# Block 0's queries in slots of the weight ring, and new durations in the planner of a fused attention and two-MLP kernel

## The chip, the cores and the metric

The kernel runs on one core of one Trainium2 chip. The time of a kernel is its device time in microseconds (us). Engines are named as in the profile: PE is TensorE (matmuls), DVE is VectorE, ACT is ScalarE, POOL is GpSimd, and SP is the queue that issues most DMAs.

## What is computed

Eight batches of eight heads attend to keys and values that are pooled eight to one; the result, 4608 tokens of 512 columns, goes through two MLPs.

```python
# q, k, v: (8, 8, 576, 64)
k_p = k.reshape(B, H, Sp, pool, D).mean(axis=3)          # Sp = 72, pool = 8
v_p = v.reshape(B, H, Sp, pool, D).mean(axis=3)
attn = softmax(scale * q @ k_p^T)                        # sum + 1e-9
x = (attn @ v_p), heads side by side                     # (4608, 512)
h = x @ w_in                                             # 512 -> 2048
g = where(h >= 1, h, where(h <= -1, 0, (h + 1)**2 / 4))
x = g @ w_out                                            # 2048 -> 512
out = (sigmoid(x @ w_gate) * (x @ w_val)) @ w_out2       # 512 -> 1536 -> 512
```

## The kernel before

The weights of the MLPs come as 64-bit floating-point numbers. The kernel reads them as pairs of 32-bit words, makes float32 of them on ACT and DVE (`weight`), and splits every operand of a main matmul into a high and a low float32r part. `three` multiplies high by high, high by low and low by high, so one product of a 128 x 128 tile with 512 columns is three matmuls.

The tokens are nine blocks of 512 (`j`). Attention is done per block and pair of heads (`unit(j, p)`, four pairs); `pooled(b, p)` makes the pooled keys and values of batch b. For block 0 the keys and values are summed on PE and the queries are transposed on PE (lines 384 to 389); for the later blocks queries come in 32 x 32 pieces by many small DMAs and are transposed on DVE (lines 395 and 401).

The first MLP runs as 144 steps, nine blocks of 16 column tiles of w_in (`M1`). A step makes h (12 matmuls), then g on ACT and DVE (lines 645 to 649, then `high_part` and `low_part`, lines 505 and 514), then adds to four accumulators (12 matmuls). During block 0 the weights arrive and are converted: a tile of w_in is loaded into a slot of the ring "win" (16 slots), converted through f, and its two float32r parts take another slot of "win"; a tile of w_out is loaded into the ring "raw" (two slots) and kept as float32, and split again in each step (`wj`). The attention of block j + 1 is done during block j. The second MLP follows: block 0 in a plain way, with the weights combined into seven sums and differences on the side, and the other eight blocks in four pairs with seven products for eight. Their due times go by `S2` and `PSTEP`.

Nothing is issued in the order of the code. Every instruction, or small group, is recorded with `op(engine, cost, key, function, r=, w=)`: the engine or the engines that could do it, its duration in us, a due time (the key), and the buffers that it reads and writes. `Plan.issue` then runs a list scheduler over them while the program is built: it follows its own clock, lets an engine start what is ready, of several that are ready within 0.05 us the one with the lowest key, gives an operation that two engines could do to the one that would end it first, and takes a slot of a ring for a buffer when one is free by that clock. A DMA lasts, in the plan, by its `nbytes` at 360 GB/s behind the ones before it, with at most eight under way. What comes out is the fixed order of each engine's queue; on the chip every queue works in that order and waits for semaphores.

So the costs decide the order of the queues and which of ACT and DVE does a copy; they do not decide what is computed. Keys for the steps are `due1(s) = 30 + 6.35 s`. The load of w_in's tile m has the key due1(m) - 0.1 - 23.19, that of w_out's tile m due1(m + 1) - 2.73 - 23.19. In block 0, pair p of the attention has T = 2.02 p; its k and q loads have the key T - 20, its v load T + 10.09. The pairs of block 1 have T = due1(2), due1(4), due1(7), due1(10), each less 6.12, and their k and q loads the key T - 20.

Buffers of a ring are recorded by `Buf`; one with `fifo=False` need not take its slot in the recorded order. In the kernel before the four q tiles of block 0 and those of all later blocks share the ring "q", which has two slots:

```python
qs = buf_a("q", 2, [P, NT4, 2, D])        # block 0, line 376
qs = buf_a("q", 2, [P, TB // 32, 32])     # later blocks, line 391
```

Of the kernel before, what the change touches and what calls it, by code (L numbers as in the profile page):

```python
# [18 lines left out]
P = 128  # L19
# [177 lines left out]
def pooled_attention_two_mlps(  # L197
# [92 lines left out]
    T0, S1, S2 = START, STEP1, 7.8  # L290

    def due1(s):
        return T0 + S1 * s
# [69 lines left out]
    def unit(j, p, T):  # L363
# [53 lines left out]
        for h in range(2):  # L417
# [4 lines left out]
            op(DVE, 0.37, T + 4, lambda view=view, mx=mx: nc.vector.tensor_reduce(  # L422
# [16 lines left out]
        if first:  # L439

            flat = Src(aT, lambda t: t.rearrange("c a h t j -> c (a h t j)"))
            for h in range(2):
# [9 lines left out]
                op((ACT, DVE), (0.48, 0.6), T + 10, (  # L452
                    lambda copy=copy: copy(nc.scalar.copy),
                    lambda copy=copy: copy(nc.vector.tensor_copy)), r=[pt], w=[aT])
        else:
            aq = buf_a("aq", 1, [P, 3, 2, NT4 * 32])
            for h in range(2):
                op(DVE, 0.47, T + 9, lambda h=h: nc.vector.transpose(
                    out=aq.t[:, :, h].rearrange("p b (t j) -> p t b j", t=NT4),
                    in_=e.t[:, :, h].rearrange("p t (b i) -> p t b i", i=32)), r=[e], w=[aq])  # L460
# [28 lines left out]
        op((ACT, DVE), (0.48, 0.6), T + 19 - AHEAD_PX * first, (  # L489
# [3 lines left out]
        op(DVE, 0.6, T + 19 - AHEAD_PX * first, lambda: nc.vector.scalar_tensor_tensor(  # L493
# [8 lines left out]
    def high_part(key, dst, src, eng=None):  # L502

        ways = {
            ACT: (0.52, lambda: nc.scalar.copy(out=dst.t[:, 0], in_=src())),  # L505
            DVE: (0.34, lambda: nc.vector.tensor_copy(out=dst.t[:, 0], in_=src())),
            PL: (0.59, lambda: nc.gpsimd.tensor_scalar(
                out=dst.t[:, 0], in0=src(), scalar1=1.0, scalar2=1.0, op0=ALU.mult, op1=ALU.mult))}
        engs = eng or HI
        op(engs, [ways[e][0] for e in engs], key, [ways[e][1] for e in engs], r=[src.b], w=[dst])  # L510

    def low_part(key, dst, src, eng=None):
        engs = eng or LO
        op(engs, [0.6 if e == DVE else 1.23 for e in engs], key, [lambda e=e: by[e].tensor_tensor(  # L514
# [12 lines left out]
    def weight(w, m, cols, r, key, t=None, keep=None, spill=None):  # L527
# [23 lines left out]
        op(ACT, 0.52, key - 7, lambda: nc.scalar.activation(out=f.t, in_=high().bitcast(F32), func=AF.Abs),  # L551
           r=[r], w=[f])
        a = op(ACT, 0.52, key - 6, lambda: nc.scalar.activation(
            out=low().bitcast(I32), in_=low(), func=AF.Copy, scale=2.0 ** -29), r=[r])
# [3 lines left out]
        op(DVE, 0.34, key - 5, lambda: nc.vector.tensor_scalar(  # L558
            out=f.t.bitcast(U32), in0=f.t.bitcast(U32), scalar1=3, scalar2=0x3FFFFFF8,
            op0=ALU.logical_shift_left, op1=ALU.bitwise_and), r=[f], w=[f])  # L560
        op(DVE, 0.6, key - 5, lambda: nc.vector.scalar_tensor_tensor(
# [22 lines left out]
    def columns(key, o, w, xs):  # L584
        last = []
        for c in range(KD):
# [30 lines left out]
    for j in range(NB):  # L617
        xs = xs_of.pop(j)
        for m in range(M1):
# [39 lines left out]
            for c in range(KD):  # L659
# [3 lines left out]
                last_y[c] = [op(PE, 0.65, due1(s + 2) + 2.6 + 0.1 * c, mm, r=[wj, g], w=[accs[c]], behind=last_y[c])]  # L663
# [45 lines left out]
    PSTEP = 11 * 2.6  # L709
# [20 lines left out]
    def prepare(n, i, key):  # L730
# [19 lines left out]
        def comb(o, x, y, alu):  # L750
            op2(DVE, 0.38, key - 4, lambda: nc.vector.tensor_tensor(out=sm.t[:, o], in0=x(), in1=y(), op=alu),
# [27 lines left out]
    def out_part(gs, m, key, accs, last, ahead=5):  # L779
# [5 lines left out]
        for c in range(4):  # L785
# [3 lines left out]
            last[c] = [op(PE, 0.65, key + 0.1 * c, mm, r=[w, g], w=[accs[c]], behind=last[c])]  # L789
# [13 lines left out]
    for i in range(MP):  # L803
# [3 lines left out]
        for n in range(2):  # L807
            sl, a21 = slots[n]
            for f in range(2):
                last = []  # L810
                for c in range(KD):
# [5 lines left out]
                    last = [op(PE, 0.65, T + 5.2 * n + 2.6 * f + 0.1 * c, mm, r=[sl, a21, xs[c]], w=[banks[n, f]], behind=last)]  # L817
# [11 lines left out]
    for pr in range(NPR):  # L829
# [45 lines left out]
        for i in range(MP):  # L875
            sig = {}
            for n in range(2):
# [4 lines left out]
                def product(pos, o, mat, xx, start, sl=sl):  # L882
# [5 lines left out]
                    op(PE, 1.3, T + H * pos, mm, r=[sl] + xx + ([] if start else [o]), w=[o])  # L888
# [81 lines left out]
```

## Time and profile before

| | us |
|---|---|
| median of 3 runs | 1756.39 (1753.28 to 1759.51) |
| the profiled execution, device time | 1755.67 |
| its span, first to last instruction | 1753.8 |
| PE busy in the span | 1723.8 (98%) |
| DVE busy | 1051.5 (60%) |
| ACT busy | 805.7 (46%) |

The span holds the whole kernel: attention of block 0 and the first weights, then 144 steps of the first MLP, then the second MLP. Busy time of PE counts matmuls from their start to a modelled end, so a PE that is busy all the time can still be fed a little slower than it could be. An engine's wait is put down to the instruction that released it last.

### The profile page before, as it was taken

Reading aid. Unit: us, or ns where it says so; the run is one execution under the profiler, and the core shown is the slowest. Engines: PE = TensorE matmul, PEld = TensorE weight load, DVE = VectorE, ACT = ScalarE, POOL = GpSimd, SP = SyncE. Lnnn points to the kernel's source line nnn. Section 1 sums busy time; section 2 is a strip of 40 time slices with the busy share of each in tenths; the row PEclk is TensorE's granted clock in tenths of the full one; section 3 lists DMA queues with packets and bytes.
Section 4 is the critical chain, followed back from the end, with each engine's and each line's share of the span. In section 5 each row is a group of like instructions: output and inputs, shape, how many; then the busy total and the mean of one; then the engine's idle time right before and its main releaser. Section 6 shows DMA issues by size and latency. Waiting matters only on the chain.

```text
span 1753.8 us, 24039 instructions
## 1 busy us (share of the span) xinstructions
PE 1723.8 (98%) x9016; PEld 1393.4 (79%) x9016; DVE 1051.5 (60%) x1874; ACT 805.7 (46%) x1786; POOL 52.7 (3%) x90
## 2 busy tenths in 40 slices
PE   7899999999999999999999999999999999999998
PEld 5676777778777778777887888888888888888887
DVE  5899867677776867574646645345444644464432
ACT  5876656566665656564755332123222312141212
POOL 0000001010010101010000000000000000000000
PEclk9999999999999999999999999999999999999999
DMA  7742525243443414031415875354344433443411
GB/s 205 229 119 69 149 57 163 62 134 97 116 116 92 134 45 134 16 128 40 174 39 202 318 291 204 126 192 145 126 146 166 149 119 146 166 167 126 150 43 49
DMA packets 148532, 234.37 MB, mean 134 GB/s; under 512 B 84160, under 2 KB 104640, under 8 KB 140736
## 3 DMA queue, kind: packets, MB, share of 16 engines
q1 hardware_dynamic: 138624, 182.50, 33.1%
q0 software_dynamic: 9792, 50.34, 7.9%
q8 instruction: 71, 1.16, 0.3%
q14 instruction: 45, 0.37, 0.1%
HBM read 173.02 MB, written 50.33 MB: 127 GB/s over the span
## 4 chain that ended last, share of the span: by engine, by line
PE 92%; DMA 3%; DVE 2%; ACT 1%; SPq 0%; issue 0%; DVEq 0%; ACTq 0%
PE acc L580 13%; PE h L580 13%; PE acc L582 13%; PE acc L581 13%; PE h L582 13%; PE h L581 12%; PE a L582 4%; PE a L581 4%; PE a L580 4%; PE a L484 2%; DMA raw<-in_moe_w_out_dram 1%; PE a L413 1%; DMA kv<-in_v_dram 1%; DMA x<-in_v_dram 1%; DMA xb<-y 0%
## 5 line engine op out<-in xcount | busy, mean ns | idle before, releaser
L580 PE MATMUL h<-x,win 128*128 128x512 f32 x576 | 231.2, 401 | 1.0 <-ACT win L505 1.0
L580 PE MATMUL acc<-g,wj 128*128 128x512 f32 x576 | 228.7, 397 | 1.2 <-ACT g L505 1.2
L582 PE MATMUL acc<-g,wj 128*128 128x512 f32 x576 | 225.4, 391 | 3.5 <-DVE wj L514 3.5
L582 PE MATMUL h<-x,win 128*128 128x512 f32 x576 | 225.7, 392 | 1.3 <-DVE win L514 1.3
L581 PE MATMUL acc<-g,wj 128*128 128x512 f32 x576 | 225.6, 392 | 1.0 <-DVE g L514 1.0
L581 PE MATMUL h<-x,win 128*128 128x512 f32 x576 | 225.5, 391 | 0.0
L781 ACT CAST g<-gs 128x512 fp32r<-128x512 f32 x108 | 66.8, 622 | 319.2 <-PE acc L582 200.4
L645 ACT ACTIVATE t<-h,half 128x512 f32<-128x512 f32 x144 | 99.2, 689 | 186.9 <-PE h L582 186.9
L582 PE MATMUL acc<-win,g 128*128 128x512 f32 x432 | 168.2, 389 | 2.1 <-DVE g L782 2.1
L580 PE MATMUL acc<-win,g 128*128 128x512 f32 x432 | 168.2, 389 | 0.0
L581 PE MATMUL acc<-win,g 128*128 128x512 f32 x432 | 168.1, 389 | 0.0
L782 DVE TENSOR_TENSOR g<-gs,g 128x512 fp32r<-128x512 f32 x108 | 74.1, 690 | 135.2 <-ACT g L781 135.0
L649 DVE SCALAR_TENSOR_TENSOR t<-t,h 128x512 f32<-128x512 f32 x144 | 97.3, 676 | 90.9 <-ACT t L647 90.8
L580 PEld LDWEIGHTS h<-x,win 128*128 128x128 f32 x576 | 108.7, 189 | 35.7 <-issue 9.7
L582 PEld LDWEIGHTS acc<-g,wj 128*128 128x128 f32 x576 | 108.4, 188 | 28.4 <-DVE wj L514 5.4
L580 PEld LDWEIGHTS acc<-g,wj 128*128 128x128 f32 x576 | 108.2, 188 | 27.8 <-ACT g L505 1.7
L582 PEld LDWEIGHTS h<-x,win 128*128 128x128 f32 x576 | 108.7, 189 | 25.9 <-DVE win L514 2.5
L581 PEld LDWEIGHTS acc<-g,wj 128*128 128x128 f32 x576 | 108.3, 188 | 23.2 <-DVE g L514 1.6
L581 PEld LDWEIGHTS h<-x,win 128*128 128x128 f32 x576 | 108.8, 189 | 21.1
L514 DVE TENSOR_TENSOR wj<-wout_f,wj 128x512 fp32r<-128x512 f32 x144 | 99.0, 688 | 33.3 <-ACT wj L505 33.0
L514 DVE TENSOR_TENSOR g<-t,g 128x512 fp32r<-128x512 f32 x144 | 98.8, 686 | 33.6 <-ACT g L505 33.1
L505 ACT CAST g<-t 128x512 fp32r<-128x512 f32 x144 | 89.1, 619 | 52.5 <-DVE t L649 50.1
(212 smaller groups left out, 3231.1 us busy)
## 6 DMA issues: line engine op xcount, KB each, us to landing
wa<-seven SPq DMA_DIRECT2D x32, 1792.0 KB
wb<-seven SPq DMA_DIRECT2D x16, 1792.0 KB
seven<-wa POOLq DMA_DIRECT2D x8, 1792.0 KB, 7.4
y<-raw SPq DMA_DIRECT2D x18, 512.0 KB
w<-f POOLq DMA_DIRECT2D x36, 256.0 KB, 2.5
out_dram<-raw SPq DMA_DIRECT2D x18, 512.0 KB
win<-in_moe_w_in_dram SPq DMA_DIRECT2D x16, 512.0 KB
raw<-in_moe_w_out_dram SPq DMA_DIRECT2D x16, 512.0 KB
```

Source lines behind the costliest of these rows:

```text
L413: nc.tensor.matmul(out=scs[h].t[r0 % P:r0 % P + D, r0 // P * C:r0 // P * C + C], lhsT=qT.t[D * h:D * h + D, r0:r0 + D], rhs=kts[b % 2, p]. ...
L484: nc.tensor.matmul(out=px.t[D * h:D * h + D, lo:hi], lhsT=vps[b % 2, p].t[:, h], rhs=rhs, start=True, stop=True)
L505: ACT: (0.52, lambda: nc.scalar.copy(out=dst.t[:, 0], in_=src())),
L514: op(engs, [0.6 if e == DVE else 1.23 for e in engs], key, [lambda e=e: by[e].tensor_tensor(out=dst.t[:, 1], in0=src(), in1=dst.t[:, 0].bi ...
L580: nc.tensor.matmul(out=o, lhsT=wh, rhs=xh, start=start, stop=False, skip_group_check=more)
L581: nc.tensor.matmul(out=o, lhsT=wh, rhs=xl, start=False, stop=False, skip_group_check=more)
L582: nc.tensor.matmul(out=o, lhsT=wl, rhs=xh, start=False, stop=stop, skip_group_check=more)
L645: op(ACT, 0.69, Tg, lambda t=t, hps=hps: nc.scalar.activation(out=t.t, in_=hps.t, func=AF.Relu, bias=half.t, scale=0.5), r=[hps, half], w=[t])
L649: op(DVE, 0.69, Tg + 2, lambda t=t, hps=hps: nc.vector.scalar_tensor_tensor(out=t.t, in0=t.t, scalar=1.0, in1=hps.t, op0=ALU.min, op1=ALU. ...
L781: op2(ACT, 0.62, key - ahead, lambda: nc.scalar.copy(out=g.t[:, 0], in_=gs.t), r=[gs], w=[g])
L782: op2(DVE, 0.69, key - ahead + 1, lambda: nc.vector.tensor_tensor(out=g.t[:, 1], in0=gs.t, in1=g.t[:, 0].bitcast(F32), op=ALU.subtract), r ...
```

## The change

The four q tiles of block 0 no longer use the ring "q"; each takes a slot of "win", the ring of the weights of the first MLP. The `nbytes` of their loads is halved (to the bytes that they have). The durations of most operations on DVE and ACT are raised by some 0.1 us each, that of three matmuls from 0.65 to 0.68 (and 1.3 to 1.36 for six), and the due times of the second MLP are stretched to match: `S2` from 7.8 to 8.16, `PSTEP` from 11 x 2.6 to 11 x 2.72. All other constants and all keys of the first MLP stay. The core of the diff (the operations left out change their cost in the same way):

```diff
-    T0, S1, S2 = START, STEP1, 7.8
+    T0, S1, S2 = START, STEP1, 8.16
...
-            qs = buf_a("q", 2, [P, NT4, 2, D])
+            qs = Buf(win_p, "win", M1, [P, NT4, 2, D], fifo=False)
             for h in range(2):
                 op(SP, 0.475, T - 20, lambda h=h: nc.sync.dma_start(
-                    out=qs.t[:, :, h], in_=q[0, h0 + h, 0:TB].rearrange("(s t) d -> s t d", t=NT4)), w=[qs], nbytes=TB * D * 8)
+                    out=qs.t[:, :, h], in_=q[0, h0 + h, 0:TB].rearrange("(s t) d -> s t d", t=NT4)), w=[qs], nbytes=TB * D * 4)
...
-            op((ACT, DVE), (0.48, 0.6), T + 1, (
+            op((ACT, DVE), (0.59, 0.69), T + 1, (
...
-            op(DVE, 0.6, T, lambda: nc.vector.transpose(out=qT.t, in_=qs.t.rearrange("p t i -> p (t i)")),
+            op(DVE, 0.7, T, lambda: nc.vector.transpose(out=qT.t, in_=qs.t.rearrange("p t i -> p (t i)")),
...
-            op(DVE, 0.37, T + 4, lambda view=view, mx=mx: nc.vector.tensor_reduce(
+            op(DVE, 0.46, T + 4, lambda view=view, mx=mx: nc.vector.tensor_reduce(
...
-            ACT: (0.52, lambda: nc.scalar.copy(out=dst.t[:, 0], in_=src())),
-            DVE: (0.34, lambda: nc.vector.tensor_copy(out=dst.t[:, 0], in_=src())),
+            ACT: (0.62, lambda: nc.scalar.copy(out=dst.t[:, 0], in_=src())),
+            DVE: (0.43, lambda: nc.vector.tensor_copy(out=dst.t[:, 0], in_=src())),
...
-        op(engs, [0.6 if e == DVE else 1.23 for e in engs], key, [lambda e=e: by[e].tensor_tensor(
+        op(engs, [0.69 if e == DVE else 1.23 for e in engs], key, [lambda e=e: by[e].tensor_tensor(
...
-        op(ACT, 0.52, key - 7, lambda: nc.scalar.activation(out=f.t, in_=high().bitcast(F32), func=AF.Abs),
+        op(ACT, 0.68, key - 7, lambda: nc.scalar.activation(out=f.t, in_=high().bitcast(F32), func=AF.Abs),
...
-        op(DVE, 0.34, key - 5, lambda: nc.vector.tensor_scalar(
+        op(DVE, 0.43, key - 5, lambda: nc.vector.tensor_scalar(
...
-            last = [op(PE, 0.65, key + 0.1 * c, mm, r=[w, xs[c]], w=[o], behind=last)]
+            last = [op(PE, 0.68, key + 0.1 * c, mm, r=[w, xs[c]], w=[o], behind=last)]
...
-    PSTEP = 11 * 2.6
+    PSTEP = 11 * 2.72
...
-                    op(PE, 1.3, T + H * pos, mm, r=[sl] + xx + ([] if start else [o]), w=[o])
+                    op(PE, 1.36, T + H * pos, mm, r=[sl] + xx + ([] if start else [o]), w=[o])
```

## Rows read from the trace of the kernel before

**Rows 1.** The page's engine totals: busy us, share of the span, instructions.

```profile
PE 1723.8 (98%) x9016; PEld 1393.4 (79%) x9016; DVE 1051.5 (60%) x1874; ACT 805.7 (46%) x1786; POOL 52.7 (3%) x90
```

**Rows 2.** Busy time of each engine by stage; stretch and length first.

```profile
core 0: us, PE busy (x) PEld busy (x) DVE busy (x) ACT busy (x) POOL busy (x), PEclk, DMA share, GB/s
0.00:10.00 10.00, 5.67 (x70) 5.02 (x71) 0.76 (x2) 2.30 (x4) 0.69 (x6) 1.00 0.69 185
10.00:20.00 10.00, 5.58 (x132) 4.96 (x130) 5.03 (x13) 7.04 (x37) 0.00 (x0) 0.87 0.96 256
20.00:40.00 20.00, 18.10 (x181) 14.13 (x182) 13.37 (x31) 9.61 (x42) 0.00 (x0) 0.90 0.72 168
40.00:160.00 120.00, 109.22 (x754) 82.38 (x753) 110.37 (x223) 91.16 (x224) 0.00 (x0) 0.97 0.55 157
...
200.00:900.00 700.00, 700.00 (x3956) 556.45 (x3956) 475.76 (x905) 426.81 (x1023) 44.48 (x71) 1.00 0.35 99
1000.00:1100.00 100.00, 100.00 (x443) 82.84 (x442) 49.77 (x78) 27.62 (x46) 1.60 (x3) 1.00 0.64 240
```

**Rows 3.** Waits of PE: total us, times, longest.

```profile
PE acc L384 <- DMA q<-in_q_dram: 5.5, 1, 5.5
...
PE acc L582 <- DVE wj L514: 3.5, 4, 1.8
...
PE h L580 <- ACT win L505: 1.0, 1, 1.0
...
PE acc L582 <- DVE g L782: 2.1, 1, 2.1
```

**Rows 4.** SP's issues in order of time: start us, us, count.

```profile
5.56 0.41 SPq L543 DMA_DIRECT2D win<-in_moe_w_in_dram  x1
...
8.94 3.78 SPq L378 DMA_DIRECT2D q<-in_q_dram  x2
...
15.05 3.90 SPq L378 DMA_DIRECT2D q<-in_q_dram  x2
...
20.62 1.65 SPq L543 DMA_DIRECT2D win<-in_moe_w_in_dram  x2
...
23.25 15.28 SPq L395 DMA_DIRECT2D q<-in_q_dram  x16
38.57 1.58 SPq L543 DMA_DIRECT2D win<-in_moe_w_in_dram  x3
```

**Rows 5.** Instructions in order of time, idle time before them in brackets.

```profile
13.57 0.67 ACT L551 ACTIVATE f<-win 128x512 f32<-128x512 f32 x1 [2.16 <-DMA win<-in_moe_w_in_dram]
...
22.19 0.69 DVE L389 COPY qT<-acc 128x512 f32<-128x512 f32 x1 [3.47 <-PE acc L384]
...
24.88 0.32 ACT L425 ACTIVATE g<-a,mx 128x72 f32<-128x72 f32 x1 [4.71 <-DVE mx L422]
...
36.03 0.71 DVE L401 STREAM_TRANSPOSE qT<-q 128x512 f32<-128x512 f32 x1 [3.57 <-DMA q<-in_q_dram]
...
38.22 0.75 DVE L432 TENSOR_TENSOR g<-g,sm 128x576 f32<-128x576 f32 x1
...
46.63 0.48 PE L580 MATMUL h<-x,win 128*128 128x512 f32 x1
```

**Rows 6.** DMA issues of the whole kernel: count, KB each.

```profile
q<-in_q_dram SPq DMA_DIRECT2D x32, 56.0 KB
...
x<-in_k_dram SPq DMA_DIRECT2D x4, 288.0 KB
...
q<-in_q_dram SPq DMA_DIRECT2D x8, 128.0 KB
```

**Rows 7.** Groups by line, shapes apart: count, busy us, mean ns, idle before.

```profile
L514 DVE TENSOR_TENSOR wj<-wout_f,wj 128x512 fp32r<-128x512 f32 x144 | 99.0, 688 | 33.3 <-ACT wj L505 33.0
...
L556 DVE TENSOR_SCALAR f<-f 128x512 f32<-128x512 f32 x68 | 28.4, 421 | 5.5 <-ACT f L551 5.5
```

**Rows 8.** Block 1's pair 3 in order of time: its scores, its x.

```profile
114.63 0.73 PE L413 MATMUL a<-kt,qT 64*64 64x72 f32 x32
...
141.43 0.69 DVE L493 SCALAR_TENSOR_TENSOR x<-a,x 128x512 fp32r<-128x512 f32 x1
```

More of the change, by code (lines that the diff above doesn't have):

```diff
@@ L428, in unit @@
                     accum_out=sums.t[:, t, h:h + 1]), r=[sc, mx], w=[e, sums], after=[zeros])
-        op(DVE, 0.07, T + 8, lambda: nc.vector.tensor_scalar(
+        op(DVE, 0.17, T + 8, lambda: nc.vector.tensor_scalar(
             out=sums.t, in0=sums.t, scalar1=1e-9, scalar2=None, op0=ALU.add), r=[sums], w=[sums])
-        op(DVE, 0.12, T + 8, lambda: nc.vector.reciprocal(out=sums.t, in_=sums.t), r=[sums], w=[sums])
+        op(DVE, 0.2, T + 8, lambda: nc.vector.reciprocal(out=sums.t, in_=sums.t), r=[sums], w=[sums])
         op(DVE, 0.75, T + 8, lambda: nc.vector.tensor_tensor(
@@ L451, in copy @@
                     eng(out=flat()[:, TB * h:TB * h + TB], in_=pt.t[:C])
-                op((ACT, DVE), (0.48, 0.6), T + 10, (
+                op((ACT, DVE), (0.59, 0.69), T + 10, (
                     lambda copy=copy: copy(nc.scalar.copy),
@@ L457, in unit @@
             for h in range(2):
-                op(DVE, 0.47, T + 9, lambda h=h: nc.vector.transpose(
+                op(DVE, 0.57, T + 9, lambda h=h: nc.vector.transpose(
                     out=aq.t[:, :, h].rearrange("p b (t j) -> p t b j", t=NT4),
@@ L488, in unit @@
            r=[aT] + [vps[b % 2, p] for _, _, b, _ in segs], w=[px], share=C / P)
-        op((ACT, DVE), (0.48, 0.6), T + 19 - AHEAD_PX * first, (
+        op((ACT, DVE), (0.59, 0.69), T + 19 - AHEAD_PX * first, (
             lambda: nc.scalar.activation(out=x.t[:, 0], in_=px.t, func=AF.Copy, scale=1.0 / POOL),
@@ L492, in unit @@
                 out=x.t[:, 0], in0=px.t, scalar1=1.0 / POOL, scalar2=None, op0=ALU.mult)), r=[px], w=[x])
-        op(DVE, 0.6, T + 19 - AHEAD_PX * first, lambda: nc.vector.scalar_tensor_tensor(
+        op(DVE, 0.69, T + 19 - AHEAD_PX * first, lambda: nc.vector.scalar_tensor_tensor(
             out=x.t[:, 1], in0=px.t, scalar=1.0 / POOL, in1=x.t[:, 0].bitcast(F32),
@@ L549, in weight @@
         f = Buf(f_p, "f", 3, [P, DM])
[L551 removed]
+        op(ACT, 0.68, key - 7, lambda: nc.scalar.activation(out=f.t, in_=high().bitcast(F32), func=AF.Abs),
            r=[r], w=[f])
[L553 removed]
+        a = op(ACT, 0.68, key - 6, lambda: nc.scalar.activation(
             out=low().bitcast(I32), in_=low(), func=AF.Copy, scale=2.0 ** -29), r=[r])
[L556 removed]
+        op(DVE, 0.43, key - 5, lambda: nc.vector.tensor_scalar(
             out=f.t, in0=f.t, scalar1=mag_lo, scalar2=mag_hi, op0=ALU.max, op1=ALU.min), r=[f], w=[f])
[L558 removed]
+        op(DVE, 0.43, key - 5, lambda: nc.vector.tensor_scalar(
             out=f.t.bitcast(U32), in0=f.t.bitcast(U32), scalar1=3, scalar2=0x3FFFFFF8,
             op0=ALU.logical_shift_left, op1=ALU.bitwise_and), r=[f], w=[f])
[L561 removed]
+        op(DVE, 0.69, key - 5, lambda: nc.vector.scalar_tensor_tensor(
             out=f.t.bitcast(U32), in0=high(), scalar=0xC0000000, in1=f.t.bitcast(U32),
@@ L595, in out_rows @@
             for n, a in enumerate(accs[2 * i:2 * i + 2]):
-                op((ACT, DVE), (0.48, 0.6), key, (
+                op((ACT, DVE), (0.59, 0.69), key, (
                     lambda st=st, a=a, n=n: nc.scalar.copy(out=st.t[:, n], in_=a.t),
@@ L662, in mm @@
                           g.t[:, 0], g.t[:, 1], m == 0, m == M1 - 1)
-                last_y[c] = [op(PE, 0.65, due1(s + 2) + 2.6 + 0.1 * c, mm, r=[wj, g], w=[accs[c]], behind=last_y[c])]
+                last_y[c] = [op(PE, 0.68, due1(s + 2) + 2.6 + 0.1 * c, mm, r=[wj, g], w=[accs[c]], behind=last_y[c])]
             one_ops += plan.ops[n0:]
@@ L750, in comb @@
         def comb(o, x, y, alu):
-            op2(DVE, 0.38, key - 4, lambda: nc.vector.tensor_tensor(out=sm.t[:, o], in0=x(), in1=y(), op=alu),
+            op2(DVE, 0.42, key - 4, lambda: nc.vector.tensor_tensor(out=sm.t[:, o], in0=x(), in1=y(), op=alu),
                 r=[sl, a21] + ([sm] if o else []), w=[sm])
@@ L788, in mm @@
                       w.t[:, 0], w.t[:, 1], m == 0, m == M2 - 1)
-            last[c] = [op(PE, 0.65, key + 0.1 * c, mm, r=[w, g], w=[accs[c]], behind=last[c])]
+            last[c] = [op(PE, 0.68, key + 0.1 * c, mm, r=[w, g], w=[accs[c]], behind=last[c])]
     def buf_gs():
@@ L816, in mm @@
                         three(o.t, a[0], a[1], xs[c].t[:, 0], xs[c].t[:, 1], c == 0, c == KD - 1)
-                    last = [op(PE, 0.65, T + 5.2 * n + 2.6 * f + 0.1 * c, mm, r=[sl, a21, xs[c]], w=[banks[n, f]], behind=last)]
+                    last = [op(PE, 0.68, T + 5.2 * n + 2.6 * f + 0.1 * c, mm, r=[sl, a21, xs[c]], w=[banks[n, f]], behind=last)]
         for f in range(2):
```

## The prediction

> **What bounds the kernel now.** I read the page's line of engine totals first, then the busy time by stage, then who waited for whom, and last the order of time in the first 50 us. The totals leave little: TensorE (PE) is busy 1723.8 of 1753.8 us [rows 1], so 30.0 us is all its idle time. By stage [rows 2], PE is busy 700.00 of 700 us from 200 to 900 us and 100.00 of 100 between 1000 and 1100, where 443 matmuls take 0.2257 us each. No order of the other engines can shorten such a stretch; the longest wait after 200 us is 2.1 us [rows 3]. What an order can still win lies ahead of 200 us: 4.33 us in the first ten, 4.42 in the second, 1.90 from 20 to 40 and 10.78 from 40 to 160 [rows 2].
>
> The second thing to see in [rows 2] is VectorE (DVE): from 40 to 160 us it is busy 110.37 of 120 us, 92%, while it turns the 32 weight tiles of the first MLP into pairs of float32r, makes the pairs of block 0's steps and does the attention of block 1. That work must be done before block 1 can run, whatever the order. So ahead of 160 us DVE sets the pace, not PE, and a microsecond in which DVE idles early is paid for at the end, unless there was nothing it could have done. From 10 to 40 us DVE idles 4.97 + 6.63 = 11.6 us.
>
> Why it idles stands in [rows 4] and [rows 5]. The queue SP issues the loads of q for pairs 2 and 3 only at 8.94 and 15.05 us, behind w_in's first tile (5.56), because the ring "q" has two slots; the queue is held 3.78 and 3.90 us by them. PE waits 5.5 us for the first [rows 3]. DVE waits 3.47 us to copy the transpose of it, and ScalarE (ACT) 4.71 us before the exponentials of pair 2, which begin at 24.88. Later DVE waits 3.57 us with line 401, the transpose of block 1's q, at the head of its queue. Behind that stand the sums and the product (line 432) of pair 3, which runs only at 38.22, and behind pair 3 the last input of step 0: PE's unbroken run of main matmuls begins at 46.63.
>
> **The change, part by part.** *The four q tiles in slots of "win".* They no longer wait for each other. By the keys in the code SP then takes k and q of all pairs (-20 to -13.94) before w_in's tile 0 (6.71) and v of pair 0 (10.09). They are 4 x 288 KB and 8 x 128 KB [rows 6], 2.23 MB. At the 185 GB/s of the first 10 us and the 256 of the next 10 [rows 2], 1.85 MB are there at 10 us and the rest at 11.5 us (an estimate). In the profile the third q was transposed and could be copied at 22.19. So PE's 5.5 us and DVE's 3.47 us go, and ACT's 4.71. What becomes late next is w_in's tile 0: 4 x 128 KB more go ahead of it, 0.52 MB at 256 GB/s = 2.0 us. ACT took that tile at 13.57, after a wait for it [rows 5], so it takes it near 15.6. Step 0 needs it before 46.63 less the microseconds won, so PE does not see the 2.0 us; but DVE has that much less to fill its gaps with.
>
> *The ring "q" is left to block 1.* Its first pair's eight loads have the key 16.58, just below w_out's tile 1 (16.78), and no longer follow block 0's q. They should land before DVE comes to line 401: the 3.57 us go, and pair 3's product moves up. The lower bound is nothing, if the plan moves line 401 forward by as much as the loads. The sixteen small loads of up to 56 KB [rows 6] held SP for 15.28 us, and w_in's fourth tile came behind them, at 38.57 [rows 4]. Eight of them now go ahead of w_in's tiles 2 and 3, issued at 20.62, and put these back by half of it, 7.6 us, to 28.2. Tile 2 is wanted one step, 24 x 0.2257 = 5.4 us, behind 46.63. With the start 5.0 us earlier that is 47.0; the 18.8 us in between hold its transfer and its conversion, some seven instructions of 0.42 to 0.69 us [rows 7], so I cost it at nothing; without that cover it is 7.6 us. The Trainium skill, "DMA: Bandwidth & Descriptors", section "Rules for kernel authors", has a rule against this part: under 64 KB a transfer is paying mostly overhead. The trace agrees, since such a load held SP 0.95 us in [rows 4]; were the weights the limit here, the sum below would be 7.6 us higher, 1756.8.
>
> So the loads give DVE back between 0 and 3.47 + 3.57 = 7.0 us. I take 7.0 less the 2.0 us by which the first weights come later: 5.0 us. It is nearer to the upper end because ACT gains 4.71 us at the same place, and both engines share what pairs 2 and 3 have to do.
>
> *nbytes halved on those loads.* No instruction changes; the plan books 0.36 us less for each of eight (131 KB at its 360 GB/s), 2.9 us together, where the trace moved 256 GB/s. It makes the plan expect q still earlier than it comes. I cost it at nothing, because PE has block 0's pooled sums of k for those microseconds; without that cover it is a wait of at most 2.9 us.
>
> *The costs.* They move no work, only the order and the choice between ACT and DVE. The old ones are low where the engine is full: 0.6 for 688 ns (line 514), 0.34 for 421 (line 556) [rows 7], and 0.65 for 3 x 0.2257 = 0.677 on PE. A plan that holds DVE 13 to 19% too short puts instructions at the head of a queue before their input is there. PE's waits between 45 and 200 us are seven groups, from 3.5 to 1.0 us, 11.7 us together [rows 3]. Both ends: all of them gone, -11.7 us, or as many again, +11.7, since another order has waits of its own. Five of the seven are for DVE's results or ACT's behind them, and DVE stays full, so I take little: -1.5 us. From 200 us on PE has almost no idle time to give. S2 and PSTEP stretch due times by 4.6% as PE's cost does (7.8 to 8.16, 2.6 to 2.72): nothing, covered by the full PE; if the cover goes, the 2.1 us at the change of stage is the size of it.
>
> **The sum.** The profiled execution took 1755.67 us, 1753.8 of span and 1.9 around it. 1755.67 - 5.0 - 1.5 = 1749.2. The median of the runs shown, 1756.39, is 0.7 above that execution; against it the sum is 1749.9. I give 1749.5.
>
> **The rivals.** *Hidden anyway* (1753 to 1758 us). DVE gets pairs 2 and 3 earlier, but then idles for weights, because the link sets the pace and the change takes no byte away: 185 to 256 GB/s in the first 20 us. For it: ACT did wait for w_in's first tile. Against it: at 38.57 SP was still issuing tiles that no engine had missed, and from 40 us on DVE is 92% full.
>
> *Slower: block 1's last pair comes late* (about 1762 us). The border between block 0 and block 1 is open only when pair 3 of block 1 has been through attention: its scores run on PE at 114.63 and its x is finished by DVE from 141.43 on [rows 8]. These 27 us lie in DVE's full stage. The higher costs show the plan that DVE is full, and then it ranks by key; if it puts conversions of weights ahead of this chain, PE has no step of block 1 to do while it lasts. Two steps of 5.4 us, 10.8 us later, less the 5.0 won, is 5.8 and 1761.5; it is slower from two steps on, and one step costs what the loads win. For it: DVE is the engine whose costs rise most in sum. Against it: keys are the same as before, and pair 3's (from 87.4) are ahead of those of the last steps of block 0.
>
> *A better order pays more* (about 1742 us). 5.0 from the loads and 8 to 9 of the 11.7 us of waits. For it: ACT is busy only 91.16 of 120 us from 40 to 160 [rows 2], so true costs can shift copies to it. Against it: the costs of both engines rise by about the same share, so most choices stay.
>
> *The change does not do what it says*: the win ring runs short and w_in's tiles wait for the q tiles' slots. There are sixteen, and the q tiles are read before the fourth w_in tile is even issued. I give it no chance of its own.
>
> **How the numbers follow.** Forecast 0.45 (1746 to 1753), hidden 0.28, slower 0.15, better order 0.12. A measurement of this kernel tells 0.3%, 5.3 us, from no change: faster is below 1751.1, slower above 1761.7. Of the forecast's band 0.41 lies below 1751.1, with the better order that is 0.53. The same is the hidden case, 0.28, with 0.04 of the forecast and 0.02 of the slower case, 0.34; slower is the other 0.13. The range runs from 1741, a better order, to 1759, part way to the slower case; it leaves out most of that case and gains beyond 15 us. The likeliest case's own range is 1746 to 1753.
>
> **What the profile after would show.** SP issues all eight loads of q ahead of w_in's first tile. PE's wait of 5.5 us for q is gone. Pair 2's exponentials begin some 5 us before 24.88. DVE's idle time from 10 to 40 us falls from 11.6 to about 6, with no wait of line 401 in front of pair 3's product. PE's unbroken run begins some 5 us before 46.63, and block 1's pair 3 is finished by as much before 141.43. PE stays full from 200 to 900. I am wrong if DVE idles between 40 and 100 us for weights, or if PE's waits after 45 us grow by more than the 5 us won.

## The result and the profile after

| | before | after |
|---|---|---|
| median, us | 1754.49 (1750.88 to 1761.37, 7 runs) | 1771.81 (1767.78 to 1779.09, 7 runs) |
| ratio, 95% interval | 1 | 1.0102 (1.0086 to 1.0117) |
| span of the profiled execution, us | 1753.8 | 1777.3 |

The kernel is 1.0% slower, where 1749.5 us and a gain were forecast; the range ended at 1759. The profiled execution took 1779.09 us, the longest of the seven, so the rows below show some 7 us more than the median does. Of the runs in the next section, one execution of costs_dma (2464.69 us) and one of both_moved (9856.44 us), far from all others of the same kernel, are left out of the ratios, not of the medians.

The engine totals of the changed kernel, beside [rows 1]:

```profile
PE 1744.7 (98%) x9016; PEld 1405.7 (79%) x9016; DVE 1050.4 (59%) x1871; ACT 806.1 (45%) x1789; POOL 52.2 (3%) x90
```

The work is the same, and PE still fills its span: 20.9 us more of busy time for the same 9016 matmuls. So it ran slower for a while. Where, the busy time by stage shows (columns as in [rows 2]):

```profile
0.00:10.00 10.00, 4.35 (x44) 3.53 (x48) 0.76 (x2) 2.10 (x3) 0.70 (x6) 1.00 0.72 180
10.00:20.00 10.00, 10.00 (x172) 8.62 (x174) 4.20 (x10) 6.11 (x35) 0.00 (x0) 1.00 0.98 262
20.00:40.00 20.00, 15.14 (x116) 12.43 (x116) 9.80 (x25) 6.98 (x36) 0.00 (x0) 0.73 0.78 168
40.00:60.00 20.00, 20.00 (x98) 13.92 (x95) 9.39 (x19) 10.03 (x19) 0.00 (x0) 0.50 0.93 298
...
200.00:900.00 700.00, 697.73 (x3974) 553.29 (x3973) 479.08 (x921) 426.04 (x1039) 45.29 (x73) 1.00 0.36 102
```

From 40 to 60 us PE is busy 20.00 of 20 us and does 98 matmuls at a granted clock of 0.50, the lower of its two levels (1.2 instead of 2.4 GHz). DVE, busy 110.37 of 120 us from 40 us on in [rows 2], is busy 9.39 of these 20 us, and 9.80 of the 20 before (13.37 in the kernel before). From 200 us on all is nearly as in the kernel before. The waits of PE, and SP's issues, beside [rows 3] and [rows 4]:

```profile
PE acc L353 <- DVE aT L451: 4.9, 1, 4.9
PE acc L332 <- DMA x<-in_k_dram: 4.3, 1, 4.3
PE acc L582 <- DVE wj L514: 3.9, 4, 1.6
...
PE acc L384 <- DMA win<-in_q_dram: 1.3, 1, 1.3
```

```profile
7.47 1.21 SPq L378 DMA_DIRECT2D win<-in_q_dram  x2
8.73 1.00 SPq L543 DMA_DIRECT2D win<-in_moe_w_in_dram  x1
...
15.15 13.01 SPq L395 DMA_DIRECT2D q<-in_q_dram  x8
28.20 0.48 SPq L547 DMA_DIRECT2D raw<-in_moe_w_out_dram  x1
28.72 0.98 SPq L543 DMA_DIRECT2D win<-in_moe_w_in_dram  x2
```

All eight q loads go ahead of w_in's first tile, and PE's wait for q falls from 5.5 to 1.3 us: this part did what it says. Block 1's eight small loads go from 15.15 to 28.16 us. The timeline shows what became of it, beside [rows 5]:

```profile
29.96 0.71 DVE L401 STREAM_TRANSPOSE qT<-q 128x512 f32<-128x512 f32 x1 [7.75 <-DMA q<-in_q_dram]
30.60 1.24 DVE L451 COPY aT<-acc 72x512 f32<-72x512 f32 x2
...
31.30 7.10 PE L353 MATMUL acc<-x,ident 72*72 72x128 f32 x32 [4.86 <-DVE aT L451]
...
32.30 0.32 ACT L425 ACTIVATE g<-h,mx 128x72 f32<-128x72 f32 x1 [8.80 <-DVE mx L422]
...
47.63 7.03 PE L353 MATMUL acc<-x,ident 72*72 72x128 f32 x32
...
58.20 0.80 PE L580 MATMUL h<-x,win 128*128 128x512 f32 x1
```

Line 401 is now at the head of DVE's queue ahead of the copies of block 0's aT, not behind pair 2's product, and waits 7.75 us for the small loads, not 3.57. DVE comes to it at 22.21 us, some 10 us sooner than in the kernel before (32.46); the data comes at 29.96, 6.1 us sooner. Behind it wait PE (4.86 us at line 353) and, through pair 3's maxima (line 422), ACT (8.80 us). And the clock falls, in windows of 2 and 4 us:

```profile
26.00:28.00 2.00, 0.44 (x4) 0.18 (x2) 0.00 (x0) 0.00 (x0) 0.00 (x0) 1.00 0.48 62
28.00:30.00 2.00, 0.00 (x0) 0.00 (x0) 0.04 (x1) 0.00 (x0) 0.00 (x0) 0.84 0.51 109
30.00:32.00 2.00, 0.70 (x3) 0.70 (x4) 2.00 (x4) 0.00 (x0) 0.00 (x0) 0.50 0.93 304
...
58.00:62.00 4.00, 4.00 (x11) 2.82 (x9) 3.37 (x6) 2.79 (x5) 0.00 (x0) 0.50 1.07 383
62.00:64.00 2.00, 2.00 (x35) 1.47 (x35) 0.36 (x1) 0.00 (x0) 0.00 (x0) 0.63 1.09 394
```

It falls while PE stands idle, and comes back at 62 to 64 us, some 4 us after step 0 has begun. In between the 32 matmuls of line 353 take 7.03 to 7.10 us; the kernel before does such a group, at 29.64, in 3.66. PE's unbroken run begins at 58.20, not at 46.63 [rows 5].

To compare runs I count main matmuls of line 582, one for each three, ended by 240 us: 221 before, 191 after. These 30 stand for 30 x 3 x 0.2257 = 20.3 us, most of the 23.5 us between the spans. Most of the loss is made ahead of 240 us.

### The profile page after: what moved, and what is told of

It is laid out like the page before. It is cut to its first block, busy times and chain, and to the rows that moved or that the text cites. A ratio compares the mean times of both kernels' runs of the same rounds, so it can differ in the third digit from the quotient of the medians.

```text
span 1777.3 us, 24059 instructions
## 1 busy us (share of the span) xinstructions
PE 1744.7 (98%) x9016; PEld 1405.7 (79%) x9016; DVE 1050.4 (59%) x1871; ACT 806.1 (45%) x1789; POOL 52.2 (3%) x90
## 4 chain that ended last, share of the span: by engine, by line
PE 89%; DMA 4%; issue 2%; DVE 2%; SPq 2%; ACT 1%; DVEq 0%; POOL 0%; POOLq 0%
PE h L580 12%; PE acc L580 12%; PE acc L582 12%; PE acc L581 12%; PE h L582 12%; PE h L581 12%; PE a L582 4%; PE a L580 4%; PE a L581 4%; PE a L484 2%; PE a L413 1%; DMA kv<-in_k_dram 1%; PE acc L353 1%; SPq L464 1%; DMA kv<-in_v_dram 1%
## 5 line engine op out<-in xcount | busy, mean ns | idle before, releaser
L582 PE MATMUL acc<-g,wj 128*128 128x512 f32 x576 | 225.9, 392 | 4.1 <-DVE wj L514 3.9
L582 PE MATMUL h<-x,win 128*128 128x512 f32 x576 | 226.2, 393 | 0.9 <-DVE win L514 0.9
L582 PE MATMUL acc<-win,g 128*128 128x512 f32 x432 | 168.3, 390 | 0.6 <-DVE g L782 0.4
L582 PEld LDWEIGHTS acc<-g,wj 128*128 128x128 f32 x576 | 108.4, 188 | 30.2 <-DVE wj L514 7.1
L582 PEld LDWEIGHTS h<-x,win 128*128 128x128 f32 x576 | 109.1, 189 | 25.1 <-DVE win L514 1.5
L505 ACT CAST wj<-wout_f 128x512 fp32r<-128x512 f32 x144 | 89.0, 619 | 48.5 <-PE acc L582 45.7
```

The lines of the kernel that those rows point to most:

```text
L505: ACT: (0.62, lambda: nc.scalar.copy(out=dst.t[:, 0], in_=src())),
L582: nc.tensor.matmul(out=o, lhsT=wl, rhs=xh, start=False, stop=stop, skip_group_check=more)
```

## The experiments

The columns: median; ratio to the kernel before on the same chip, with its interval; line 582's matmuls by 240 us in its trace. The diffs below show the lines, or parts of lines, that matter; the setting up of the lists that they use (`freed`, `spare`, `held`, `loads`, `back`, `kept`, `gone`) is left out.

| run | us | ratio | L582 |
|---|---|---|---|
| slots_only | 1764.67 | 1.0053 (1.0032 to 1.0073) | 216 |
| costs_only | 1768.52 | 1.0078 (1.0063 to 1.0094) | 204 |
| q1_late | 1767.90 | 1.0073 (1.0055 to 1.0091) | 205 |
| fill20 | 1770.69 | 1.0087 (1.0065 to 1.0108) | 201 |
| l401_moved | 1768.75 | 1.0081 (1.0065 to 1.0097) | 205 |
| costs_wout3 | 1765.74 | 1.0063 (1.0047 to 1.0079) | 206 |
| q1_late_wout3 | 1765.40 | 1.0070 (1.0045 to 1.0094) | 208 |
| dma260_q4 | 1750.75 | 0.9978 (0.9968 to 0.9987) | 231 |
| before_dma | 1758.14 | 1.0023 (1.0010 to 1.0037) | 228 |
| slots_dma | 1753.41 | 1.0005 (0.9994 to 1.0017) | 226 |
| costs_dma | 1758.39 | 1.0024 (1.0013 to 1.0035) | 223 |
| dma260 | 1763.96 | 1.0056 (1.0039 to 1.0073) | 212 |
| both_moved | 1764.46 | 1.0053 (1.0039 to 1.0066) | 211 |
| wout_moved | 1771.73 | 1.0094 (1.0077 to 1.0110) | 202 |
| costs_wout_moved | 1768.01 | 1.0077 (1.0061 to 1.0092) | 207 |
| three_moved | 1769.27 | 1.0083 (1.0067 to 1.0099) | 201 |
| costs_kv_moved | 1770.95 | 1.0096 (1.0080 to 1.0112) | 200 |
| costs_kv_wout_moved | 1772.74 | 1.0101 (1.0085 to 1.0117) | 205 |

### Each part alone

**slots_only** is the kernel before with block 0's q in "win" and the halved nbytes:

```diff
-            qs = buf_a("q", 2, [P, NT4, 2, D])
+            qs = Buf(win_p, "win", M1, [P, NT4, 2, D], fifo=False)
...
-  w=[qs], nbytes=TB * D * 8)
+  w=[qs], nbytes=TB * D * 4)
```

> Only the q tiles in slots of win, with the halved nbytes; all costs and due times as before. Theory (line 401 at the head of DVE's queue): the early loads of block 1's q alone put line 401 ahead of block 0's copies, so it waits 5 to 9 us, PE runs dry and its granted clock falls: 1762 to 1775 us. Rival (the new costs did it): no such harm, the forecast's gain of some 5 us shows, 1745 to 1752 us.

1764.67 us, as the theory had it: the slots alone cost some 9 us. Line 401 stands ahead of block 0's aT copies here too:

```profile
29.66 0.71 DVE L401 STREAM_TRANSPOSE qT<-q 128x512 f32<-128x512 f32 x1 [6.98 <-DMA q<-in_q_dram]
```

**costs_only** is the rest of the change (all durations, `S2`, `PSTEP`) with the ring "q" as it was.

> Only the new costs and due times; q of block 0 in its own ring of two as before. Theory (line 401): block 1's q is loaded as late as before, line 401 waits no longer than the 3.57 us of before, and the time is within 6 us of before, 1748 to 1760 us. Rival (the new costs did it): as slow as the whole change, 1765 to 1775 us.

1768.52 us, the rival's number: the new durations cost more than the slots, some 13 us where -1.5 was forecast. The two sum to 1.3%, more than the change's 1.0%; the intervals are too wide to show that they cover each other. Line 582 is level with the kernel before at 60 us, 11 behind at 90 and 17 behind at 240. In that first and largest stretch the trace waits at pair 2 of block 1 (SP's queue, then PE):

```profile
55.20 11.15 SPq L395 DMA_DIRECT2D q<-in_q_dram  x8
66.47 0.40 SPq L547 DMA_DIRECT2D raw<-in_moe_w_out_dram  x1
67.39 1.78 SPq L395 DMA_DIRECT2D q<-in_q_dram  x4
69.27 0.48 SPq L313 DMA_DIRECT2D kv<-in_k_dram  x1
```

```profile
73.34 2.19 PE L332 MATMUL a<-ident,kv 72*64 72x72 f32 x32 [5.25 <-DMA kv<-in_k_dram]
```

PE waits 5.25 us for keys whose load stands behind twelve small q loads. ACT too waits in this run, 3.99 us at line 551 for a tile of w_out; nine tiles of w_in had gone to SP in one run, from 38.40 us.

### Line 401, the clock, and the wait behind them

**q1_late** lets the small loads of block 1's pairs 0 and 1 go only after block 0's pairs 2 and 3 have been transposed (`freed` holds those transposes), as the ring did before:

```diff
-                op(SP, 0.475, T - 20, lambda f=f: load_q(f), w=[qs], nbytes=TB * 256, dmas=len(segs))
+                op(SP, 0.475, T - 20, lambda f=f: load_q(f), w=[qs], nbytes=TB * 256, dmas=len(segs), after=freed[2 + p:3 + p] if j == 1 and p < 2 else [])
```

> The whole change, but the plan may issue the q loads of block 1's pairs 0 and 1 only after the transposes of block 0's q of pairs 2 and 3, so w_out's tile 1 and w_in's tiles 2 and 3 go first again and line 401 comes later in DVE's queue. Theory (line 401): PE's 4.9 us wait for aT and the half clock from 30 to 62 us go: 1745 to 1757 us. Rival (the new costs): nothing changes, 1765 to 1775 us.

**fill20** keeps the changed kernel's order and adds 20 matmuls, whose result nothing reads, to PE's queue ahead of its wait at line 353:

```diff
+                    for _ in range(20 if (p, h) == (1, 1) else 0): nc.tensor.matmul(out=spare[0].t[:, 384:512], lhsT=ident.t, rhs=ident.t, start=True, stop=True)
```

> The whole change with every queue in its order, and twenty matmuls of the identity more on PE, into unused columns of a bank, in front of its wait for aT: they add no result, they only keep PE at work from 26.4 to about 31 us. Line 401 waits as long as in the change. Theory (the larger part of the loss is the half clock after the wait): the granted clock stays near 1 from 30 to 62 us and PE's work there takes about half: 1755 to 1763 us. Rival (the loss is the wait itself and the new order, the clock only shows it): 1768 to 1775 us.

**l401_moved** keeps every queue of the changed kernel but issues block 1's first line 401 behind the product (line 432) of block 0's pair 3:

```diff
-            op(DVE, 0.7, T, lambda: nc.vector.transpose(
+            op(DVE, 0.7, T, (lambda: held.append((qT, qs))) if (j, p) == (1, 0) else lambda: nc.vector.transpose(
...
-            in1=sums.t.unsqueeze(3).to_broadcast([P, NT4, 2, C]), op=ALU.mult),
+            in1=sums.t.unsqueeze(3).to_broadcast([P, NT4, 2, C]), op=ALU.mult), held_401() if (j, p) == (0, 3) else None),
```

> The whole change with every queue in its order but for one instruction: line 401 of block 1's first pair stands in DVE's queue behind the product of block 0's pair 3, sixteen instructions later. Theory (two waits: line 401 with the half clock behind it, then ACT's wait for w_out behind w_in's tiles): the first goes, PE's first steps come some 15 us earlier than in the change, and ACT's wait of 6 to 8 us for w_out gives half of that back: 1758 to 1766 us. Rival (line 401 only shows a start that is late anyway): 1768 to 1775 us.

In fill20 and l401_moved the clock is 1.00 from 20 to 40 us, and step 0 begins early: by 60 us line 582 has done 12 matmuls in either, 13 in the kernel before, 1 in the changed one. In q1_late PE's wait at line 353 is gone too, but line 401 still waits 4.49 us. Yet all three times are the rivals': 1.0073, 1.0087 and 1.0081 beside 1.0102 give back at most 5 of the 18 us. Each run loses time at the same load, which the rows of ACT show, for q1_late, fill20 and l401_moved:

```profile
60.29 0.66 ACT L551 ACTIVATE f<-raw 128x512 f32<-128x512 f32 x1 [6.50 <-DMA raw<-in_moe_w_out_dram]
```

```profile
60.93 0.66 ACT L551 ACTIVATE f<-raw 128x512 f32<-128x512 f32 x1 [7.66 <-DMA raw<-in_moe_w_out_dram]
```

```profile
58.98 0.66 ACT L551 ACTIVATE f<-raw 128x512 f32<-128x512 f32 x1 [9.42 <-DMA raw<-in_moe_w_out_dram]
```

ACT stands with line 551 at the head of its queue for w_out's tile 2, which SP issued behind five w_in tiles (three in q1_late); behind it in ACT's queue stands what PE waits for: the exponentials in fill20 and l401_moved, g of line 505 in q1_late (7.83 us). SP, then PE, in l401_moved:

```profile
46.20 4.10 SPq L543 DMA_DIRECT2D win<-in_moe_w_in_dram  x5
50.41 1.85 SPq L547 DMA_DIRECT2D raw<-in_moe_w_out_dram  x1
```

```profile
61.88 2.19 PE L332 MATMUL a<-ident,kv 72*64 72x72 f32 x32 [7.68 <-ACT e_sb L425]
```

In the changed kernel step 0 begins late, and ACT waits only 2.1 us in all for w_out's tiles from 40 to 150 us: the late start covers this wait. Of the 16 to 20 of line 582's matmuls that these runs lack by 240 us, 5 to 7 are lost only after 140 us; what costs these is not shown.

### The second wait away as well

**costs_wout3** and **q1_late_wout3** make the plan issue w_in's tile m only after w_out's tile m - 3, in costs_only and in q1_late. The term added to that load's `behind`:

```diff
+ behind=r.behind + (loads[2 * (m - 3) + 1:2 * (m - 3) + 2] if spill is None and cols and m >= 3 else [])
```

> The new costs alone, as in costs_only, and one rule more for the plan: the load of w_in's tile m goes after that of w_out's tile m - 3. In costs_only nine tiles of w_in went ahead of w_out's tile 2. Theory (two waits): what costs_only lost, 12 us between steps 2 and 4, was ACT at the head of its queue with w_out's tile, and PE's wait for block 1's k behind the same tiles; it goes, 1748 to 1759 us. Rival (the new costs harm by the order of ACT and DVE): as costs_only, 1764 to 1771 us.

> q1_late with the same rule for w_in's loads. Theory (two waits): PE's 7.8 us wait for g goes as well and the earlier start is kept: 1744 to 1755 us. Rival (order of ACT and DVE): 1763 to 1770 us, as q1_late.

1.0063 and 1.0070 against 1.0078 and 1.0073: not clearly better, and both the rivals' numbers, so these two runs leave open whether the order of ACT and DVE does the harm. ACT's wait of 4 us and more is gone; PE waits instead 5.6 us in all for "win" (line 514) in the one and 5.8 us for wj in the other. These edits let the plan choose another order, so three more keep every queue of the changed kernel but for named instructions. **wout_moved** puts w_out's tiles 2 and 3 ahead of the five and four w_in tiles on SP, **both_moved** does that and l401_moved's edit, **three_moved** puts tile 4 ahead of w_in's 12 to 15 as well (other counts in the dictionary). The edit in both of the first two:

```diff
- key - AHEAD_LOAD, load, w=[r]
+ key - AHEAD_LOAD, (lambda: back.append(load)) if w is w_in and m > 6 else lambda: (load(), [back.pop(0)() for _ in range({2: 5, 3: 4}.get(m, 0) if w is w_out else 0)]), w=[r]
```

> Every queue as in the changed kernel, but for three places: block 1's first line 401 stands behind block 0's last pair on DVE, and on SP the loads of w_out's tiles 2 and 3 stand ahead of the five and the four w_in tiles that they followed. Theory (the two waits, DVE's for the early small q loads and ACT's for w_out's tile, are the whole loss, and each hid the other): step 0 starts as in the run with line 401 alone moved, 2.5 us ahead of the kernel before at the eighth matmul group, ACT's wait of 9.42 us at line 551 shrinks to under 2 us, and the time is 1754 to 1760 us. Rival 1 (the w_in tiles that are put back by a w_out tile each are now what is late, as in the runs with the plan's order held to three tiles): waits of PE for win or wj of 4 us and more, 1763 to 1768. Rival 2 (the loss lies in the order of the other instructions): 1768 to 1770, as with line 401 alone moved.

> As the changed kernel, line 401 where it was; only the loads of w_out's tiles 2 and 3 stand ahead of the w_in tiles that they followed. Theory (in the changed kernel the late start covers the wait for w_out): 1769 to 1773 us, the same as the changed kernel within its spread, with the half clock from 30 to 62 us and PE's 4.9 us wait at line 353 as they were. Rival (w_out's tile costs the changed kernel its time, and the clock nothing): 1760 to 1764.

> As the run with both moved, and the load of w_out's tile 4 stands ahead of w_in's tiles 12 to 15 too. With both moved, PE led the kernel before by 1.5 us in step 3 and lost 7 us in step 4, where ACT stood 5.16 us at line 553 for tile 4. Theory (that wait is the rest of the loss that lies in the first MLP's start): tile 4 lands some 5 us earlier, ACT's wait falls under 2 us, and the time is 1756 to 1760 us. Rival (the transfers are the limit there, and whichever tile comes last is waited for): PE waits for win instead, 1763 to 1766, as with two tiles moved.

wout_moved comes out like the changed kernel, as the late start's cover would have it, though in its trace the clock is back by 50 us and not, as expected, by 62. both_moved gives back half of the loss, 1.0053 against 1.0102. That is not the theory's 1754 to 1760 but rival 1's number, and PE's waits for wj sum to 6.5 us. But w_in's tiles are not what is late (PE's wait for win is 0.8 us): w_out's are. ACT's waits for w_out in both_moved:

```profile
51.05 0.66 ACT L551 ACTIVATE f<-raw 128x512 f32<-128x512 f32 x1 [2.55 <-DMA raw<-in_moe_w_out_dram]
...
59.64 0.68 ACT L551 ACTIVATE f<-raw 128x512 f32<-128x512 f32 x1 [3.97 <-DMA raw<-in_moe_w_out_dram]
...
69.55 0.67 ACT L553 ACTIVATE raw<-raw 128x512 int32<-128x512 uint32 x1 [5.16 <-DMA raw<-in_moe_w_out_dram]
```

The 9.42 us became 2.55, and the next two tiles became late. In three_moved the last of these ends 4 us earlier, at 65.48, yet the time falls back to 1769.27: now ACT waits for the tile after, and PE for the rows of aT, whose loads SP began only at 71.17, behind four w_in tiles and six small q loads:

```profile
79.47 0.66 ACT L551 ACTIVATE f<-raw 128x512 f32<-128x512 f32 x1 [5.46 <-DMA raw<-in_moe_w_out_dram]
```

```profile
80.75 1.76 PE L484 MATMUL a<-aT,vp 72*64 72x64 f32 x8 [4.01 <-DMA aT<-aq]
```

With the durations alone it goes the same way. **costs_wout_moved** moves w_out's tiles 2 and 3 in costs_only, **costs_kv_moved** puts the twelve small q loads behind pair 2's keys, **costs_kv_wout_moved** does both:

```diff
- lambda f=f: load_q(f), w=[qs]
+ lambda f=f: kept.append(lambda: load_q(f)) if j == 1 and p > 1 and not gone else load_q(f), w=[qs]
...
- lambda: load(k, ks), w=[ks]
+ lambda: (load(k, ks), (gone.append(1), [x() for x in kept]) if (b, p) == (1, 2) else None), w=[ks]
```

> The new durations alone, ring q as before, every queue as in that run, but on SP w_out's tiles 2 and 3 go ahead of six of the nine and three w_in tiles. Theory (the durations' loss is ACT's wait for w_out's tile, some 8 to 10 us): 1757 to 1761 us against 1768.5 with the durations alone. Rival (w_in is late in its place): 1764 to 1767, as where the plan itself was held to three tiles.

> The new durations alone, every queue as in that run but SP's: twelve small q loads for block 1's pairs 2 and 3, which DVE reads only at 97 and 124 us, go behind the load of pair 2's keys instead of ahead of it. Theory (PE's 5.25 us wait at line 332 for these keys, and the lower clock behind it, are most of the 13.6 us that the durations cost): the wait is gone, 1757 to 1762 us. Rival (w_out's tile is waited for at the same place, ACT's 4 us at line 551): 1766 to 1769, as with the durations alone.

> Both changes of SP's order at once: the twelve q loads behind pair 2's keys, and w_out's tiles 2 and 3 ahead of six and three w_in tiles. Theory (the loss is what SP's queue puts last): 1755 to 1759 us. Rival (the durations' loss lies in other queues): 1764 us and more.

All three theories fell: 1768.0, 1771.0 and 1772.7 us. The first left PE's wait for the keys (4.5 us). The second left 0.7 us of it, and aT's loads came behind sixteen small q loads (9.44 us of SP from 67.40); PE waited 8.0 us for aT at line 484, and the clock was 0.60 from 80 to 100 us. The third comes out as its rival had it, that the durations' loss lies in other queues; its trace shows 4.3 us of PE for aT and 2.7 us for values. So none of the waits that were moved carries the loss alone: in each of these traces a load that is pulled ahead makes another one late. A part that lies in the order of ACT and DVE is not excluded.

### The plan's time for a DMA

What these waits would share is that the plan thinks the data has come. **dma260_q4** changes only what it believes of DMAs: 260 GB/s for 360, and four times the nbytes for block 1's small q loads.

```diff
-                    dma = max(dma, t + 0.65) + o.bytes / o.dmas / 360e3
+                    dma = max(dma, t + 0.65) + o.bytes / o.dmas / 260e3
...
-  w=[qs], nbytes=TB * 256, dmas=len(segs))
+  w=[qs], nbytes=TB * 256 * (4 if j == 1 else 1), dmas=len(segs))
```

> The whole change, and the plan is given durations of DMAs nearer to the trace too: 260 GB/s in place of 360, and block 1's small q loads four times as long. No rule on the order. Theory (what harms is a plan that believes its DMAs early while it has learnt that DVE and ACT are slow): line 401 and the w_out tiles are placed where their data is there: 1744 to 1758 us. Rival (the costs of ACT and DVE themselves): 1764 to 1775 us.

1750.75 us, within the theory's range: faster than both kernels, by 0.22% than the one before. Of its trace, the stages, then DVE at line 401, and SP:

```profile
20.00:40.00 20.00, 17.98 (x231) 12.75 (x228) 16.64 (x39) 13.20 (x47) 0.00 (x0) 1.00 0.79 188
40.00:60.00 20.00, 17.50 (x106) 13.27 (x106) 19.80 (x41) 17.90 (x45) 0.00 (x0) 1.00 0.63 189
```

```profile
33.69 0.71 DVE L401 STREAM_TRANSPOSE qT<-q 128x512 f32<-128x512 f32 x1
```

```profile
16.33 11.78 SPq L395 DMA_DIRECT2D q<-in_q_dram  x8
...
41.12 1.53 SPq L543 DMA_DIRECT2D win<-in_moe_w_in_dram  x3
45.07 0.35 SPq L547 DMA_DIRECT2D raw<-in_moe_w_out_dram  x1
45.46 3.90 SPq L395 DMA_DIRECT2D q<-in_q_dram  x6
54.33 0.35 SPq L547 DMA_DIRECT2D raw<-in_moe_w_out_dram  x1
```

The small loads still go first, from 16.33 us; but line 401 stands behind pair 3's product and waits for nothing, and SP sends w_in's tiles spread out, with w_out's between them: 189 GB/s from 40 to 60 us, where the changed kernel drew 298. DVE is busy 19.80 of these 20 us and the clock stays at 1.00.

The same DMA times went to the kernel before (**before_dma**), to it with the slots alone (**slots_dma**) and to it with the new durations alone (**costs_dma**); **dma260** is the changed kernel with the rate alone.

> The kernel before with the plan's DMA durations alone changed (260 GB/s in place of 360, block 1's small q loads four times as long). Theory (a plan that believes its DMAs early is what harms): a little faster than before or the same, 1748 to 1756 us. Rival (dma260_q4 is fast by a lucky order): no relation to before, anywhere from 1750 to 1768 us.

> q tiles in slots of win, old costs, the plan's DMA durations as in dma260_q4. Theory: with true DMAs line 401 is not put ahead of block 0's copies, so the slots do no harm: 1746 to 1754 us, not above before_dma by more than 2 us. Rival: the slots still cost 5 to 9 us, 1757 to 1765 us.

> New costs and due times, q in its own ring, the plan's DMA durations as in dma260_q4. Theory: w_out's tiles are no longer put behind nine of w_in, so the new costs do no harm: 1747 to 1756 us. Rival: the costs still lose 8 to 13 us, 1763 to 1769 us.

> The whole change with 260 GB/s in the plan, but block 1's small q loads as short as before. Theory: the w_out wait goes, line 401 may still come too early: between, 1750 to 1762 us. Rival (line 401's loads are all that matters): as the change, 1768 to 1774 us.

With them slots_only's 1.0053 becomes 1.0005, costs_only's 1.0078 becomes 1.0024, and the whole change's 1.0102 becomes 0.9978. slots_dma is in its theory's range; costs_dma and dma260 lie between theory and rival. The rate alone gives 1.0056: 0.46% of the change's loss, and the small loads' length another 0.78% behind it. But before_dma, 1.0023, is slower than the kernel before, just beyond its theory's 1756. Its rival was that dma260_q4 is fast by a lucky order. Line 582's matmuls by 240 us speak against luck there: all four kernels gain by the new DMA times, the one before from 221 to 228, the slots from 216 to 226, the durations from 204 to 223, the change from 191 to 231. What before_dma wins it loses later. At 940 us it still leads the kernel before by 6 of these matmuls, at 1100 us it is 4 behind; the second MLP begins there, and PE waits for DVE (line 701):

```profile
PE a L582 <- DVE wa L701: 2.7, 1, 2.7
```

All five runs with 260 GB/s have this wait, of 2.7 or 2.8 us, and a clock of 0.91 to 0.96 from 940 to 980 us (1.00 in the kernel before); in the other runs the wait is at most 1.2 us in all. Against before_dma the durations are worth nothing (1.0024), the slots some 0.2% and both together some 0.45%. The slots' 0.2% is not won at the first loads: slots_dma has 226 by 240 us, before_dma 228.

## Why the prediction was wrong

**The steps that failed** are two, one in each term of the sum. The first is "the 3.57 us go", under *The ring "q" is left to block 1*. Its own lower bound named the case: "if the plan moves line 401 forward by as much as the loads". The plan moved it further, by some 10 us where the data came 6.1 us sooner. The price was then not nothing but 7.75 us on DVE, 4.86 on PE, 8.80 on ACT and, in the execution shown, a clock of 0.50 for some 32 us; l401_moved, with only that instruction put back, had 12 of line 582's matmuls by 60 us where the change had 1. I bounded the wait between gone and unchanged and did not ask what a still earlier place in DVE's queue would hold up. The loads' term, -5.0, measured +9 (slots_only). The second is "I take little: -1.5 us", under *The costs*, below.

**The first loads.** Right as to q: PE's wait fell from 5.5 to 1.3 us, PE was busy 10.00 us from 10 to 20 where it had been 5.58 [rows 2], and pair 2's exponentials began at 20.42, 4.5 us sooner. The gain was gone by 30 us: DVE's idle time from 10 to 40 us went from 11.6 to 16.0 us, not to 6. ACT took w_in's first tile at 22.80, not near 15.6.

**nbytes.** Costed at nothing, with a wait of at most 2.9 us. The plan's short times for DMAs are what the last runs bear on: given longer ones it put line 401 where nothing waits for it. What the halved bytes alone did was not run apart.

**The eight small loads ahead of w_in.** They held SP 13.01 us, not half of 15.28. w_in's tiles 2 and 3 were issued at 28.72, near the forecast's 28.2, by luck: from 15.15 + 13.01, not 20.62 + 7.6. The prediction cited the Trainium skill, "DMA: Bandwidth & Descriptors", section "Rules for kernel authors": under 64 KB a transfer is mostly overhead. The trace agrees: such a load held SP 1.6 us, where its 32 KB on average (8 and 56 KB in turn) would take 0.2 us at the 168 GB/s of 20 to 40 us (an estimate). How much of the 1.6 us is the load's own is not shown; in costs_kv_moved sixteen held SP 0.6 us each. The bill came at line 401, not at w_in's tiles.

**The costs.** -1.5 was taken, between -11.7 and +11.7; costs_only is some +13 us, just beyond the upper bound. The argument was that durations nearer the trace keep instructions from standing at a queue's head. With the transfers still costed too short they did not: the new order asked SP for nine w_in tiles and twelve small loads ahead of what was needed next. That it is the mix, true engines beside fast DMAs, is what costs_dma's 1.0024 beside before_dma's 1.0023 supports: there the same durations cost nothing.

**The rivals.** *Slower* had the right sign for a reason that the trace does not show: block 1's last pair was late (its x at 160.83, not 141.43), but its other pairs were too, by 11.7 to 18.1 us, and PE's waits from 130 to 180 us are at most 2.3 us. *Better order* did not come true; even with other DMA times the change gains 0.22%, not that case's 14 us. *Hidden anyway* missed the time, but its mechanism, engines idle for weights, shows where line 401 was put back (9.42 us of ACT in l401_moved). That PE stays full from 200 to 900 us was close: 697.73 of 700.

**What stays open.** Why the longer DMA times make the plan wait at the start of the second MLP. How much of the loss lies in the order of ACT and DVE. How much of the end time the clock alone costs: where it was kept at 1.00 (fill20, to 60 us) the next wait took the time; the last section has an estimate. Whether some hand-made order of SP's queue would bring the changed kernel's other queues level: four edits by hand (l401_moved, wout_moved, both_moved, three_moved) left 0.5 to 0.9%.

## What to carry to other kernels

In a kernel whose queues come from a planner, correcting some of its durations can make it worse: here the engines' truer times beside a DMA time that was too short put waiting instructions at the heads of queues. So correct the transfers too, the small ones with them, and look at every stage: here the truer DMA times won in the first stage and lost some of it at the start of the second MLP. When a load is made earlier, look for the instruction that reads it: the plan may move that too, ahead of work that was ready. And when a hand-made repair of one wait gives back little, look in the trace for the next wait before costing another.

## What was not expected of the hardware

In the changed kernel's trace the clock stayed at 0.50 from 30 to 62 us, and PE counted as busy for 30.70 of these 32 us, mostly with matmuls of 72 and 128 columns, twice 3.68 us with those of 512 columns at line 484; it came back some 4 us into step 0. In wout_moved, with the same matmuls behind a wait of 5.66 us, it came back at 48 to 50 us, ahead of step 0. In fill20, with 20 more matmuls of 128 columns in the place of the idle time, it stayed at 1.00 from 20 to 60 us.

The executions of one kernel, with the same queues, differ with the clock: the changed one took 1767.78 us at a mean of 0.993, 1770.89 to 1771.91 at 0.991 (four of seven) and 1779.09, the execution shown, at 0.987. 11.3 us lie between the ends, and 0.006 of 1770 us is 10.6. By that slope the 0.991 beside the 0.995 of the profiled execution before would stand for some 7 of the 17 us between the medians (an estimate; whether the clock made these microseconds, or longer waits also lowered the clock, is not shown).
